# Seven half products in six pairs of chunks instead of three, and a new order, in an RWKV-6 mixer with an MLP

## The chip, the cores and the metric

The kernel runs on one core of a Trainium2 chip. The metric is the device time of one execution in microseconds (us). TensorE (PE) multiplies matrices, VectorE (DVE) and ScalarE (ACT) work on tiles and are the ones that read the accumulators (PSUM) that PE writes, GpSimd (POOL) works on tiles in SBUF, and SyncE (SP) issues the transfers (DMA). Each engine works through its own queue strictly in the order in which it was written; semaphores make it wait for others.

## The reference

```python
def _attn_ref(r, k, v, w, u):                 # [4, 8, 768, 48] each, u [8, 48]
    state = zeros(B, H, D, D)
    for t in range(S):
        cur = einsum('bhd,bhe->bhde', u * k[t], v[t])
        y[t] = einsum('bhd,bhde->bhe', r[t], state + cur)
        state = w[t][..., None] * state + einsum('bhd,bhe->bhde', k[t], v[t])
    return y
def _moe_ref(x, w_in, w_out):                 # x [3072, 384], w_in [384, 2048], w_out [2048, 384]
    h = x @ w_in
    g = np.maximum(0.01 * h, h)
    return g @ w_out
```

The y of the first part, its heads side by side, is the x of the second. Inputs and output are f32.

## The kernel before

**Chunks.** The 4 x 768 tokens are 24 chunks of 128, in an order in which consecutive chunks come from different batches, since the state passes from chunk to chunk of one batch. The first four chunks are done two at a time (`pair`, L537), the other twenty by `single` (L741). For one chunk of `single`: SP loads w, k, r and v (L755, 192 KB each) into one of ten buffers `in`; ACT takes the logarithm of w (L765); PE sums it along the tokens (L771, L774); DVE and ACT make from it the factors (L783, L792, L797, L801); DVE multiplies them with r and k (L459); the products are transposed, by PE with a copy out of PSUM (L470, L475, L477) or by a DMA transpose that SP issues (L818). PE then makes the scores (L912), DVE masks them (L842), PE multiplies them with v and adds the state's part (L878, L883). POOL makes the part of u (L489, L493, L501, with the sum L497 on DVE), casts v (L509) and scales the state (L829); DVE adds the part of u (L532), which gives y. y is transposed into xT by PE and a copy (L518, L523, L525) or by a DMA transpose that SP issues (L897).

**Blocks.** The MLP works on blocks of one or two chunks, listed in `blocks`. For a block, PE multiplies xT with w_in (the up-projection, L1074, 256 columns for a pair of chunks, 128 for a single one, six or twelve matmuls to a PSUM bank), and ACT makes g of it (L1089). Then g W_out follows in one of two forms:
- plain: per chunk 16 matmuls of 384 columns (L1104), a copy to `o` on DVE (L1115) or ACT (L1117), a store (L1121);
- seven products (`seven`, L963), for the last `SEVEN_LAST` blocks: g of a pair is cut into four quarters (two chunks, even and odd tiles of 128 features), w_out into four (even and odd tiles, left and right 192 columns). Four differences of quarters of w_out are made once on DVE (`mix`, L958). Per pair DVE makes four sums s1, s3, s2, s4 of quarters of g (L989), PE makes seven products of 8 matmuls with 192 columns (L1006) instead of eight, ACT or DVE takes three of them out of PSUM (L1020, L1022), and DVE adds five half rows into `o` (L1027: c11, f2, c21, c22, c12). The last pair makes its sums and its first products in two parts. The stores are issued at L1057.

**Order.** The kernel records about 1,100 steps, each with its engines, its estimated length and a rank, and a planner at build time (`Plan.order`) runs through them and writes the steps of each engine in the order that it finds. `RANK` adds a number to the rank of a step, and `FORCE` ties a step to one engine where several could do it. So both tables decide in what order the queues of all five engines stand, and which of DVE, ACT and POOL does a copy or a cast.

Of the kernel before, what the change touches and what calls it, by code (L numbers as in the profile page):

```python
# [23 lines left out]
class Plan:  # L24
# [138 lines left out]
RANK = {0: 15.37, 1: 14.4, 2: 3.33, 3: 23.03, 4: 38.76, 5: 12.01, 6: -26.8, 7: -21.87, 8: -21.96, 9: -19.05,  # L163
# [71 lines left out]
def kernel(  # L235
# [37 lines left out]
    SEVEN_LAST = 3  # L273
# [3 lines left out]
    blocks = [2, 1, 1, 1, 1, 2, 2, 2, 2, 2, 1, 1, 2, 2, 2]  # L277
# [903 lines left out]
```

## Time and profile before

| | |
|---|---|
| median of 3 runs | 181.93 us (181.49 to 182.0) |
| profiled execution | 181.35 us, span 179.6 us |
| busy: PE, DVE, ACT, POOL | 172.6, 132.2, 115.7, 104.0 us |
| granted TensorE clock | 1.00 |
| first up-projection, last matmul's group | starts at 19.78 us, 175.53 us |

The span goes from the first instruction to the last; the 1.75 us between it and the time of the execution lie around it. The profile gives, for each group of like instructions, its number, its busy time, the mean of one and the idle time of its engine before them. Matmuls overlap in the pipeline, so that the distance between starts says what one costs in a stream, not its mean.

### The profile page before, as it was taken

The numbers are of one execution on the slowest core, as the hardware profiler recorded it, in microseconds if no ns is written. First come the engines' busy times: TensorE is split into PE (matmuls) and PEld (weight loads), VectorE is DVE, ScalarE is ACT, GpSimd is POOL, SyncE is SP. The second block draws the span as 40 slices with busy tenths as digits, with TensorE's granted clock in tenths as the row PEclk, the third lists the DMA queues.
The fourth block names the chain that finished last, engine by engine and source line by source line (L and its number), as shares of the span: only waits on it lengthen the run. The fifth ranks groups of instructions, "written<-read, shape, count | busy, mean of one in ns | idle before, by whom it ended". The sixth has DMA issues, their size and how long they took to land.

```text
span 179.6 us, 5374 instructions
## 1 busy us (share of the span) xinstructions
PE 172.6 (96%) x2109; PEld 135.2 (75%) x2109; DVE 132.2 (74%) x265; ACT 115.7 (64%) x257; POOL 104.0 (58%) x138
## 2 busy tenths in 40 slices
PE   7998999999999999999999999999999999999991
PEld 2475878867878687787688777677778798899991
DVE  7589974189788898559687659499787599777472
ACT  2568968865957786895379775177675487735620
POOL 5989631675896486878468855414995459200000
PEclk9999999999999999999999999999999999999999
DMA  5999999999999989999899999999599996613004
GB/s 139 261 283 314 370 380 362 176 203 208 215 195 202 192 192 150 183 199 182 193 214 177 218 164 214 212 192 144 117 201 145 198 234 170 153 24 115 0 22 153
DMA packets 116715, 34.43 MB, mean 192 GB/s; under 512 B 109137, under 2 KB 115922, under 8 KB 116690
## 3 DMA queue, kind: packets, MB, share of 16 engines
q1 hardware_dynamic: 116688, 34.09, 90.8%
q8 instruction: 16, 0.26, 0.6%
q14 instruction: 9, 0.07, 0.1%
q10 hardware_dynamic: 2, 0.00, 0.0%
HBM read 25.17 MB, written 4.72 MB: 166 GB/s over the span
## 4 chain that ended last, share of the span: by engine, by line
PE 64%; DVE 8%; DMA 8%; ACT 6%; issue 5%; SPq 4%; POOL 3%; DVEq 0%; ACTq 0%; POOLq 0%
PE ps L1074 26%; PE ps L1104 17%; PE ps L1006 6%; DMA in<-in_w_dram 6%; SPq L755 3%; PE ps L1146 3%; PE ps L912 2%; DMA xT<-y 2%; DVE m L842 2%; POOL ru L489 1%; DVE o L1027 1%; ACT g L1089 1%; PE ps L883 1%; ACT rkT L477 1%; DVE m L690 1%
## 5 line engine op out<-in xcount | busy, mean ns | idle before, releaser
L1074 PE MATMUL ps<-xT,w_in_b 128*128 128x256 bf16 (+1 forms) x720 | 73.1, 251 | 0.4 <-ACT xT L525 0.2
L1089 ACT ACTIVATE g<-ps 128x512 bf16<-128x512 f32 x96 | 56.4, 595 | 20.6 <-PE ps L1074 15.3
L1074 PEld LDWEIGHTS <-w_in_b 128*128 128x128 bf16 x720 | 57.7, 98 | 9.3 <-issue 0.7
L1104 PE MATMUL ps<-w_out_b,g 128*128 128x384 bf16 x288 | 56.0, 326 | 0.1
L1104 PEld LDWEIGHTS <-g 128*128 128x128 bf16 x288 | 25.7, 97 | 12.4 <-ACT g L1089 0.2
L489 POOL TENSOR_TENSOR ru<-in,ub 128x384 f32<-128x384 f32 x24 | 24.5, 1027 | 10.9 <-DMA in<-in_k_dram 10.1
L459 DVE TENSOR_TENSOR rk<-in,ps 128x384 bf16<-128x384 f32 x46 | 24.3, 548 | 7.8 <-ACT ps L797 4.2
L842 DVE TENSOR_TENSOR m<-ps,maskb 128x512 bf16<-128x512 f32 x40 | 25.4, 683 | 6.1 <-PE ps L912 5.0
L493 POOL TENSOR_TENSOR ru<-ru,in 128x384 f32<-128x384 f32 x24 | 24.6, 1030 | 2.9 <-DMA in<-in_r_dram 2.2
L829 POOL TENSOR_TENSOR sb<-s,a 128x384 bf16<-128x384 f32 x18 | 15.7, 873 | 9.5 <-ACT a L792 9.4
L501 POOL TENSOR_TENSOR vs<-in,dg 128x384 f32<-128x384 f32 x20 | 16.6, 828 | 7.1 <-DVE dg L497 4.7
L509 POOL CAST vb<-in 128x384 bf16<-128x384 f32 x24 | 12.0, 503 | 11.3 <-DMA in<-in_v_dram 7.5
L783 DVE TENSOR_TENSOR ci<-ps,lw 128x384 f32<-128x384 f32 x20 | 11.1, 554 | 4.3 <-PE ps L771 1.9
L497 DVE TENSOR_REDUCE dg<-ru 128x8 f32<-128x384 f32 x24 | 12.9, 545 | 1.0 <-POOL ru L493 0.8
L765 ACT ACTIVATE lw<-in 128x384 bf16<-128x384 f32 x20 | 10.4, 520 | 3.6 <-DMA in<-in_w_dram 3.6
L797 ACT ACTIVATE ps<-ps 128x384 f32<-128x384 f32 x20 | 9.5, 475 | 4.2 <-DVE ci L783 3.8
L532 DVE TENSOR_TENSOR y<-ps,vs 128x384 bf16<-128x384 f32 x20 | 11.1, 553 | 1.5 <-PE ps L883 0.6
L867 DVE TENSOR_TENSOR s<-ps,sb 128x384 f32<-128x384 f32 x14 | 7.7, 552 | 4.0 <-PE ps L852 2.8
L801 ACT ACTIVATE ps<-ci 128x384 f32<-128x384 f32 x20 | 9.8, 488 | 0.6 <-DVE ci L783 0.6
L1146 PE MATMUL ps<-zeros 128*128 128x128 bf16 (+1 forms) x40 | 8.7, 339 | 1.3 <-DVE zeros L332 1.3
L525 ACT COPY xT<-ps 128x384 bf16<-128x384 bf16 x11 | 5.2, 481 | 6.8 <-PE ps L518 6.7
L792 ACT ACTIVATE a<-ps 64x4 f32<-64x4 f32 x36 | 6.0, 168 | 5.3 <-DVE ci L783 3.5
(105 smaller groups left out, 228.7 us busy)
## 6 DMA issues: line engine op xcount, KB each, us to landing
out_dram<-o SPq DMA_DIRECT2D x23, 192.0 KB, 3.2
in<-in_w_dram SPq DMA_DIRECT2D x20, 192.0 KB, 4.3
in<-in_k_dram SPq DMA_DIRECT2D x20, 192.0 KB, 4.2
in<-in_r_dram SPq DMA_DIRECT2D x20, 192.0 KB, 4.1
in<-in_v_dram SPq DMA_DIRECT2D x20, 192.0 KB, 4.3
in<-in_moe_w_out_dram SPq DMA_DIRECT2D x4, 768.0 KB, 12.3
in<-in_moe_w_in_dram SPq DMA_DIRECT2D x4, 384.0 KB, 7.0
in<-in_moe_w_in_dram SPq DMA_DIRECT2D x2, 768.0 KB, 9.8
```

The lines of the kernel that those rows point to most:

```text
L459: (nc.gpsimd if e == "POOL" else nc.vector).tensor_tensor(out=o, in0=x, in1=i, op=ALU.mult)
L489: lambda e: nc.gpsimd.tensor_tensor(out=ru.t[:], in0=kv(), in1=ubv, op=ALU.mult),
L493: lambda e: nc.gpsimd.tensor_tensor(out=ru.t[:], in0=ru.t[:], in1=rv(), op=ALU.mult),
L497: lambda e: nc.vector.tensor_reduce(out=dg.t[:], in_=ru.t[:], axis=AX.X, op=ALU.add),
L501: lambda e: nc.gpsimd.tensor_tensor(out=vs.t[:], in0=vv(), in1=dg.t[:].unsqueeze(2).to_broadcast([128, H, D]), op=ALU.mult),
L509: {"POOL": 0.56}, lambda e: nc.gpsimd.tensor_copy(out=vb.t[:], in_=vv()),
L829: lambda e: nc.gpsimd.tensor_tensor(out=sb.t[:].rearrange("p g a d -> p (g a) d"), in0=s_in.t[:].rearrange("p g a d -> p (g a) d"), in1=a_ ...
L842: lambda e, par=par: nc.vector.tensor_tensor(out=m.t[:, par, :, :], in0=sc[par].t[:].rearrange("p (g t) -> p g t", g=NP), in1=maskb[:].uns ...
L1074: nc.tensor.matmul(hp.t[:, a * N : (a + 1) * N], lhsT=w_in_b[:, t, (j + a) * 128 : (j + a + 1) * 128], rhs=xT[:, t, c0 : c0 + N], start=(a ...
L1089: lambda e, hp=hp, g=g, j=j, J=J, N=N: nc.scalar.activation(out=g.t[:, j : j + J, 0:N], in_=hp.t[:, 0 : J * N].rearrange("p (a n) -> p a n ...
L1104: nc.tensor.matmul(op.t[:, 0:DM], lhsT=g.t[:, j, off : off + 128], rhs=w_out_b[:, j, :], start=(j == 0), stop=(j == NJ - 1))
L1146: nc.tensor.matmul(warm.t[:, 0:n], lhsT=zeros[:, 0:128], rhs=zeros[:, 0:n], start=True, stop=True, skip_group_check=True)
```

## The change

Two numbers change in the kernel's body: the last six blocks, not the last three, use the seven products, and the two single blocks of chunks 16 and 17 become one pair, so that the six last blocks are pairs.

```diff
-    SEVEN_LAST = 3
+    SEVEN_LAST = 6
...
-    blocks = [2, 1, 1, 1, 1, 2, 2, 2, 2, 2, 1, 1, 2, 2, 2]
+    blocks = [2, 1, 1, 1, 1, 2, 2, 2, 2, 2, 2, 2, 2, 2]
```

The tables of the order are replaced as a whole, `RANK` with a number for nearly every step instead of for about half of them (the numbers of the steps of the MLP shift with the blocks):

```diff
-RANK = {0: 15.37, 1: 14.4, 2: 3.33, 3: 23.03, 4: 38.76, 5: 12.01, 6: -26.8, 7: -21.87, 8: -21.96, 9: -19.05,
...
+RANK = {0: -94.4, 1: -32.42, 2: -177.44, 3: -177.74, 4: 23.17, 5: -227.73, 6: -32.49, 7: -32.59, 8: -32.69, 9:
...
-FORCE = {23: "DVE", 26: "DVE", 29: "ACT", 30: "DVE", 46: "ACT", 58: "ACT", 61: "ACT", 79: "ACT", 85: "DVE",
...
+FORCE = {5: "ACT", 29: "DVE", 30: "DVE", 32: "DVE", 46: "ACT", 59: "ACT", 61: "DVE", 79: "ACT", 82: "ACT", 85:
...
```

What the two programs issue, where it differs:

| | before | after |
|---|---|---|
| L1006, 192 columns (PE) | 168 | 336 |
| L1104, 384 columns (PE) | 288 | 192 |
| L1074, 256 and 128 columns (PE) | 432 and 288 | 480 and 192 |
| L989, sums of g (DVE) | 16 | 28 |
| L1027, half sums (DVE) | 15 | 30 |
| L1115 on DVE, L1117 on ACT | 7, 11 | 2, 10 |
| L1020 on DVE, L1022 on ACT | 2, 7 | 1, 17 |
| L475 on DVE, L477 on ACT | 9, 13 | 11, 11 |

The lines of the changed kernel stand 78 further down (L1074 is L1152 there); the text goes by those of the kernel before. The pairs that use the seven products are chunks 18/19, 20/21 and 22/23 before, and all from 12/13 to 22/23 after.

More of the change, by code (lines that the diff above doesn't have):

```diff
@@ L162 @@
 TY = (0.95, 24, 0.7, -0.6)
-RANK = {0: 15.37, 1: 14.4, 2: 3.33, 3: 23.03, 4: 38.76, 5: 12.01, 6: -26.8, 7: -21.87, 8: -21.96, 9: -19.05,
[63 rows of a table removed]
-FORCE = {23: "DVE", 26: "DVE", 29: "ACT", 30: "DVE", 46: "ACT", 58: "ACT", 61: "ACT", 79: "ACT", 85: "DVE",
-    112: "DVE", 114: "ACT", 117: "DVE", 119: "ACT", 121: "ACT", 123: "DVE", 125: "POOL", 127: "ACT", 128:
-    "POOL", 134: "POOL", 137: "DVE", 139: "POOL", 142: "ACT", 143: "POOL", 492: "DVE", 500: "ACT", 604: "DVE",
-    612: "ACT", 904: "DVE", 910: "DVE", 932: "ACT", 952: "ACT", 966: "ACT", 1002: "ACT", 1030: "ACT", 1075:
-    "ACT", 1080: "ACT"}
+RANK = {0: -94.4, 1: -32.42, 2: -177.44, 3: -177.74, 4: 23.17, 5: -227.73, 6: -32.49, 7: -32.59, 8: -32.69, 9:
[138 rows of a table added]
+FORCE = {5: "ACT", 29: "DVE", 30: "DVE", 32: "DVE", 46: "ACT", 59: "ACT", 61: "DVE", 79: "ACT", 82: "ACT", 85:
+    "DVE", 86: "DVE", 112: "DVE", 114: "ACT", 115: "ACT", 117: "DVE", 127: "POOL", 128: "ACT", 130: "DVE",
+    131: "POOL", 134: "POOL", 140: "DVE", 142: "ACT", 159: "DVE", 168: "ACT", 172: "ACT", 186: "DVE", 188:
+    "ACT", 197: "ACT", 201: "DVE", 237: "DVE", 239: "DVE", 253: "ACT", 261: "DVE", 277: "ACT", 308: "DVE",
+    340: "ACT", 342: "ACT", 435: "DVE", 443: "DVE", 492: "ACT", 604: "ACT", 612: "ACT", 736: "ACT", 742:
+    "ACT", 756: "DVE", 784: "ACT", 798: "ACT", 826: "ACT", 876: "ACT", 910: "ACT", 913: "ACT", 946: "ACT",
+    949: "ACT", 982: "ACT", 985: "ACT", 990: "ACT", 1018: "ACT", 1021: "ACT", 1026: "ACT", 1054: "DVE", 1062:
+    "ACT", 1096: "ACT", 1099: "ACT", 1104: "ACT"}
 @with_exitstack
```

201 rows, old and new, of the table RANK are left out of this document.

## The prediction

> **What bounds the kernel now.** I read the page first, then the busy time of the engines by stage, then the groups of instructions by shape, and last the order of time on single engines. The page:
>
> ```profile
> PE 172.6 (96%) x2109; PEld 135.2 (75%) x2109; DVE 132.2 (74%) x265; ACT 115.7 (64%) x257; POOL 104.0 (58%) x138
> ...
> PE   7998999999999999999999999999999999999991
> ...
> PEclk9999999999999999999999999999999999999999
> ...
> PE 64%; DVE 8%; DMA 8%; ACT 6%; issue 5%; SPq 4%; POOL 3%; DVEq 0%; ACTq 0%; POOLq 0%
> ```
>
> TensorE (PE) is busy in every slice from the first to the last but one, at the full clock, and most of the chain that ended last is PE. A busy PE need not be a PE at its pace, so I ask next how often it stood idle, and what the other engines do in the same stages:
>
> ```profile
> 80.00:100.00 20.00, 19.88 (x240) 15.52 (x238) 15.88 (x32) 13.31 (x32) 13.62 (x18) 1.00 0.98 192
> 100.00:120.00 20.00, 20.00 (x211) 14.70 (x210) 14.00 (x26) 10.75 (x26) 10.11 (x13) 1.00 1.09 196
> 120.00:140.00 20.00, 19.92 (x260) 15.67 (x259) 16.60 (x30) 13.41 (x34) 14.24 (x16) 1.00 0.98 158
> 140.00:160.00 20.00, 19.91 (x249) 16.64 (x245) 15.77 (x28) 12.94 (x29) 9.26 (x12) 1.00 0.75 161
> ...
> L1104 PE MATMUL ps<-w_out_b,g 128*128 128x384 bf16 x288 | 56.0, 326 | 0.1
> L1074 PE MATMUL ps<-xT,w_in_b 128*128 128x256 bf16 x432 | 54.1, 272 | 0.4 <-ACT xT L525 0.2
> ```
>
> The columns after the length of a stretch are PE, weight loads, VectorE (DVE), ScalarE (ACT) and GpSimd (POOL). PE is full; VectorE is next with 46.4 of the 60 us from 100 to 160, 77%. The two big groups of matmuls waited 0.5 us in all. So from the first product with w_in (19.8 us) on, the end is set by the sum of PE's work, as long as the others keep ahead of it.
>
> **The change part by part.** *PE's work.* The mean of a matmul in a group is its way through the pipeline; what it costs in a full stream is the distance from one start to the next:
>
> ```profile
> 117.67 0.62 PE L912 MATMUL ps<-rkT 48*128 48x128 bf16 x16
> 118.22 1.48 PE L1074 MATMUL ps<-xT,w_in_b 128*128 128x256 bf16 x12
> ...
> 124.09 0.33 PE L878 MATMUL ps<-sb,rkT 128*128 128x96 bf16 x4
> 124.27 0.36 PE L883 MATMUL ps<-vb,m 128*128 128x48 bf16 x8
> 124.47 0.32 PE L771 MATMUL ps<-lw,trev 128*128 128x384 bf16 x1
> ...
> 124.73 3.41 PE L1104 MATMUL ps<-w_out_b,g 128*128 128x384 bf16 x20
> 127.98 0.83 PE L1074 MATMUL ps<-xT,w_in_b 128*128 128x128 bf16 x12
> 128.65 0.33 PE L852 MATMUL ps<-vb,rk 128*128 128x96 bf16 x4
> 128.82 0.83 PE L1074 MATMUL ps<-xT,w_in_b 128*128 128x128 bf16 x12
> ...
> 160.54 0.82 PE L1006 MATMUL ps<-in,in 128*128 128x192 bf16 x8
> 161.20 0.82 PE L1006 MATMUL ps<-in,g 128*128 128x192 bf16 x8
> ...
> 163.18 3.44 PE L1074 MATMUL ps<-xT,w_in_b 128*128 128x256 bf16 x30
> 166.46 0.82 PE L1006 MATMUL ps<-in,g 128*128 128x192 bf16 x8
> ```
>
> A 384-column product of the old kind (L1104) costs (127.98 − 124.73)/20 = 0.1625 us, a 192-column product of the seven (L1006) 0.66/8 = 0.0825, an up-projection of 256 columns 3.28/30 = 0.1093 and of 128 columns 0.67/12 = 0.0558. Three more pairs of chunks go from the plain form to the seven products: 3 × 32 = 96 of L1104 go (−15.60 us), 3 × 56 = 168 of L1006 come (+13.86). Chunks 16 and 17, single blocks before, become one: 96 narrow up-projections go (−5.36), 48 wide ones come (+5.25). Together −1.85 us of 160, and PE has nothing to hide it behind. This is the firm term.
>
> The Trainium skill (TensorE: Matmul & The Clock Gate, Back-to-back issue gap) speaks against it: in a stream in which each matmul has its weight load, it gives about 81 ns a matmul at 128 columns and 131 at 512. An estimate on the straight line between them is 89 ns for 192, 114 for 384, 98 for 256, so the edit would add 168 × 89 − 96 × 114 − 96 × 81 + 48 × 98 = +0.9 us instead. The trace does not agree: 55.8 ns at 128 columns and 82.5 at 192.
>
> *VectorE's work.* Per pair of chunks the seven products add four sums over g (L989, 128x1024) and five sums of halves into o (L1027); copies of o (L1115) go. In the changed order VectorE has 12 more sums, 15 more L1027 and 5 fewer L1115; the four differences of w_out (L958) come earlier, among chunks 10 to 13. What they cost beside each other:
>
> ```profile
> 143.05 2.48 DVE L842 TENSOR_TENSOR m<-ps,maskb 128x512 bf16<-128x512 f32 x4 [1.50 <-PE ps L912]
> 145.55 0.56 DVE L532 TENSOR_TENSOR y<-ps,vs 128x384 bf16<-128x384 f32 x1
> 146.02 0.55 DVE L783 TENSOR_TENSOR ci<-ps,lw 128x384 f32<-128x384 f32 x1
> 146.49 0.54 DVE L497 TENSOR_REDUCE dg<-ru 128x8 f32<-128x384 f32 x1
> ...
> 151.51 1.35 DVE L989 TENSOR_TENSOR g<-g 128x1024 bf16<-128x1024 bf16 x1
> ...
> 162.13 0.69 DVE L989 TENSOR_TENSOR g<-g 128x1024 bf16<-128x1024 bf16 x1
> 162.74 0.61 DVE L1027 TENSOR_TENSOR o<-ps,o 128x192 f32<-128x192 f32 x2
> 163.27 0.68 DVE L989 TENSOR_TENSOR in<-in,g 128x1024 bf16<-128x1024 bf16 x1
> ...
> 151.48 0.83 POOL L829 TENSOR_TENSOR sb<-s,a 128x384 bf16<-128x384 f32 x1
> ```
>
> A 384-column step costs 0.47 us (145.55 to 146.02 to 146.49), a mask 0.62, here 0.6, a half sum 0.27, here 0.28. The same sum took 0.69 us alone and 1.35 when it started beside GpSimd's L829; I price it at 0.84, nearer to the lone rows, and keep 0.6 and 1.35 as ends.
>
> I then count the queue of VectorE from y of chunk 13 to the last y (chunks 22 and 23), and PE's from the first up-projection of chunks 12/13 to that of 22/23. Before: 91 instructions, by these prices 48 us, beside 64 us of PE: 75%. After: 108 (20 masks, 54 steps of 384, 16 sums, 16 half sums, two copies into xT), 56 us. PE there has 40 groups of six wide up-projections (26.2), 32 sets of eight L1006 (21.1), 28 L1104 (4.6) and 10.7 us of small work, 62.5: VectorE is at 90%. The tightest place is behind the seven products of chunks 12/13. Their last half sum waits for PE's last product, and behind it in VectorE's queue stand 25 instructions up to y of chunk 18: 13 steps (6.1 us), 4 masks (2.4), 4 half sums (1.1), 4 sums (3.4), 13.0 us. In the same time PE goes through 9 up-projection groups (5.9), nine sets of eight L1006 (5.9) and small work of chunks 18 to 21 (L912 0.55, L878 with L883 0.38, twice L771 and what follows it 0.26, L852 0.17: 1.6), 13.4 us, and then needs that y to transpose it. Slack of 0.4 us, less the handovers, is nothing: PE waits if any of it slips. Upper end: the five sums up to y of chunk 19, all at 1.35, are 2.5 us. Lower end: −0.3, since the wide groups waited only 0.5 in the whole run. I take **+0.8 us**, a third of the upper end, for this and the like places before chunks 20/21 and 22/23; they do not add up, for a PE that waits lets VectorE gain on it.
>
> *The start.* PE's first up-projection waits for xT of both first chunks, which ACT makes last:
>
> ```profile
> 16.26 0.83 ACT L415 CAST w_in_b<-in 128x768 bf16<-128x768 f32 x1
> ...
> 17.84 0.50 ACT L734 CAST y<-ps 128x384 bf16<-128x384 f32 x1
> ...
> 18.86 0.87 ACT L525 COPY xT<-ps 128x384 bf16<-128x384 bf16 x2
> ...
> 19.78 1.47 PE L1074 MATMUL ps<-xT,w_in_b 128*128 128x256 bf16 x12
> ```
>
> After, ACT copies both y (L734) before its casts of w_in, and VectorE makes one of the two xT. That takes the cast of 0.83 and half of 0.87 out of the chain, 1.2 us at most; late is then VectorE, which does five products, a reduction and two transposed copies behind its masks before its xT, and the casts of w_in that now follow. I take **−0.5**, ends −1.0 and 0. Between 24 and 100 us PE's work is the same; loads and transposes stand in another order in SP's queue. I put nothing there, since PE waited for none of it in the row of L1074.
>
> *The end.* The last sum of halves, then a store:
>
> ```profile
> 176.39 0.36 DVE L1027 TENSOR_TENSOR o<-ps,o 128x192 f32<-128x192 f32 x1 [0.65 <-PE ps L1006]
> ...
> out_dram<-o SPq DMA_DIRECT2D x5, 192.0 KB, 1.9
> out_dram<-o SPq DMA_DIRECT2D x2, 96.0 KB, 1.6
> ```
>
> Before, the last store is a half (96 KB); after, c21 comes last and its store is whole: **+0.3 us**. PE's work behind the last up-projection stays at 6.6 us.
>
> *Sum*, on the profiled execution (181.35 us, span 179.6): 181.35 − 1.85 − 0.5 + 0.8 + 0.3 = 180.1. That execution lies 0.58 under the median of the three runs (181.93), so the time to expect of a median is **180.7 us**.
>
> **Rivals.** *VectorE becomes the bound* (slower). Place: chunks 14 to 23. For it: 90% of PE's time by rather kind prices, with each half sum waiting for a product in the middle of the same queue, and GpSimd busy for 47.2 of 80 us in the four stages above. Against: the stretch decides only from 62.5 us on, so 6.5 us of slip must come together. Price: 16 sums at 1.35 instead of 0.84 are 8.2 us, to 64.3; 2 us of waits for products and ACT make 66.3, so 3.8 us of PE standing: 180.7 − 0.8 + 3.8 = 183.7. The Trainium skill (GPSIMD Engine Reference, 1. Specifications) says that GpSimd shares its SBUF interfaces with VectorE when an instruction of the latter has two inputs there; the 1.35 beside 0.69 agrees.
>
> *The new order gives the gain back* (no change). A transpose issued by SP waits for its y or rk, and what stands behind it in that queue, loads and other transposes, waits along. One such wait of the 0.7 us by which a lone sum and one beside GpSimd differ would already outlast the slack; with nothing gained at the start, 180.7 + 0.5 + 0.7 = 181.9.
>
> *Start and middle both turn out well*: −1.0 at the start, −0.3 instead of 0.8 in the middle: 180.7 − 0.5 − 1.1 = 179.1.
>
> *The weight loads set the pace* of the seven products, so that the change saves nothing on PE. Their record is longer than the distance of the matmuls:
>
> ```profile
> L1006 PEld LDWEIGHTS <-g 128*128 128x128 bf16 x96 | 8.0, 98 | 0.5 <-ACT g L1089 0.4
> ```
>
> 168 × 0.098 = 16.5 for 15.6 is +0.9 where the sum has 13.86 − 15.60 = −1.7, so 180.7 + 2.6 = 183.3. Against it stand the 0.66 us of eight, loads included. The rule of the page on TensorE above is this rival.
>
> **How the numbers follow.** Forecast 0.58, both well 0.06, order gives it back 0.12, VectorE the bound 0.22, weight loads 0.02. A measurement of this kernel tells about 0.3% from no change, 181.4 to 182.5. So faster 0.64, same 0.12, slower 0.24. The forecast's own ends (−1.0 − 0.3 at one side, 0 and +2.5 at the other) are 179.1 and 182.9. The range for 8 in 10 goes from 178.9, under the good case, to 183.8, just over the price of the VectorE case, whose dearer half it leaves out.
>
> **What would show it.** 336 of L1006 at 0.66 us for eight, 192 of L1104: the firm term. The first up-projection before 19.5 us: the start. In the stages from 100 to 160 VectorE above 17 of 20 us, PE still above 19.7: the forecast; PE at 19 with idle put down to y or xT: the VectorE rival. L989 with a mean over 1.1 us would confirm its price. Idle on PE put down to rkT or xT by DMA would be the order's. The forecast is wrong if PE loses over 1.5 us between 100 and 165, or if the up-projections wait for weights before 36 us.

## The result and the profile after

The changed kernel takes 182.81 us (median of 20 runs, 181.37 to 185.3) beside 181.56 for the kernel before in the same measurement (20 runs, 180.32 to 183.06): a ratio of 1.007 with a 95% interval of 1.0041 to 1.0098. It is slower by 0.7%, some 1.25 us. The forecast was 180.7 us and faster. The profiled execution of the changed kernel took 182.09 us, its span 180.4. The quoted lines of the changed kernel stand 78 lower than before: L1152 is the up-projection (before L1074), L1182 the plain product (L1104), L1084 the seven products (L1006), L1067 the sums of g (L989), L1105 the half sums (L1027), L1100 the takes (L1022), L1167 the activation into g (L1089), L861 ci, L870, L875 and L879 ScalarE's exponentials, L833 the loads, L537 the products into rk, L990 the scores.

The page of the changed kernel: busy time, the row of forty slices of the DMA engines, the transfer queue, and the chain that ended last.

```profile
PE 169.2 (94%) x2126; PEld 137.8 (76%) x2126; DVE 143.3 (79%) x286; ACT 116.9 (65%) x266; POOL 106.4 (59%) x138
...
DMA  5999999998999999799998999998979978522031
...
q1 hardware_dynamic: 116688, 34.09, 91.0%
...
PE 63%; DVE 14%; DMA 7%; issue 4%; ACT 3%; POOL 3%; SPq 3%; DVEq 0%; ACTq 0%; POOLq 0%
```

PE has less work (busy 169.2 for 172.6) and the end is no earlier. VectorE's part of the chain went from 8% to 14%. The row to read twice is DMA: with few exceptions the 16 engines are at least nine tenths busy from the second slice to past 140 us, and the times of the one queue's packets add up to 91% of the 16 engines' span. It was 90.8% before, on the page that the prediction read; the prediction passes over it.

The stages from 100 us on (PE, weight loads, VectorE, ScalarE, GpSimd, clock, DMA share):

```profile
100.00:120.00 20.00, 19.72 (x252) 16.30 (x251) 17.55 (x32) 13.42 (x33) 13.02 (x16) 1.00 1.09 211
120.00:140.00 20.00, 19.21 (x247) 17.08 (x246) 18.26 (x37) 13.37 (x35) 10.33 (x13) 1.00 0.92 170
140.00:160.00 20.00, 20.00 (x249) 18.04 (x250) 17.87 (x35) 13.21 (x30) 12.72 (x14) 1.00 0.74 163
```

VectorE is at 53.7 of 60 us where it had 46.4. Of these stages PE stands idle most in the one from 120 to 140. What it waited for, in the whole run:

```profile
PE ps L548 <- DVE rk L537: 1.6, 2, 0.8
...
PE ps L930 <- POOL vb L587: 1.0, 2, 0.8
...
PE ps L1084 <- DVE o L1105: 0.7, 1, 0.7
PE ps L1084 <- ACT o L1100: 0.7, 1, 0.7
```

These are some of many small waits in different places, none of these over 0.8 us. Two can be followed by eye. In order of time, on PE and on GpSimd, with the start of the run's up-projections:

```profile
19.59 1.49 PE L1152 MATMUL ps<-xT,w_in_b 128*128 128x256 bf16 x12
...
62.69 0.33 PE L930 MATMUL ps<-vb,rk 128*128 128x96 bf16 x4 [0.77 <-POOL vb L587]
...
129.22 0.82 PE L1084 MATMUL ps<-in,in 128*128 128x192 bf16 x8 [0.66 <-ACT o L1100]
...
62.13 0.50 POOL L587 CAST vb<-in 128x384 bf16<-128x384 f32 x1 [1.99 <-DMA in<-in_v_dram]
```

At 62.69 PE waits 0.77 us for GpSimd's cast of v, which itself waits for a load. At 129.22 it waits 0.66 us for ScalarE to empty a bank of products, and that copy stands in ScalarE's queue behind work that waits for VectorE, as the experiments show. The sums themselves did not grow dear (groups of VectorE by shape):

```profile
L1067 DVE TENSOR_TENSOR in<-g,in 128x1024 bf16<-128x1024 bf16 x5 | 5.3, 1051 | 0.0
L1067 DVE TENSOR_TENSOR in<-in,g 128x1024 bf16<-128x1024 bf16 x5 | 4.1, 817 | 0.0
L1067 DVE TENSOR_TENSOR in<-g 128x1024 bf16<-128x1024 bf16 x5 | 3.8, 752 | 0.0
L1067 DVE TENSOR_TENSOR g<-g 128x1024 bf16<-128x1024 bf16 x5 | 3.4, 680 | 0.0
```

16.6 us for 20 sums are 0.83 us each; 0.84 was the price taken. So the sizes on VectorE were right and the time still went.

### The profile page after: what moved, and what is told of

Same layout as the page of the kernel before. It is cut to its first block, busy times and chain, and to the rows that moved or that the text cites. A ratio compares the mean times of both kernels' runs of the same rounds, so it can differ in the third digit from the quotient of the medians.

```text
span 180.4 us, 5448 instructions
## 1 busy us (share of the span) xinstructions
PE 169.2 (94%) x2126; PEld 137.8 (76%) x2126; DVE 143.3 (79%) x286; ACT 116.9 (65%) x266; POOL 106.4 (59%) x138
## 2 busy tenths in 40 slices
DMA packets 116716, 34.43 MB, mean 191 GB/s; under 512 B 109137, under 2 KB 115922, under 8 KB 116690
## 4 chain that ended last, share of the span: by engine, by line
PE 63%; DVE 14%; DMA 7%; issue 4%; ACT 3%; POOL 3%; SPq 3%; DVEq 0%; ACTq 0%; POOLq 0%
PE ps L1152 26%; PE ps L1084 12%; PE ps L1182 11%; DMA in<-in_v_dram 5%; DVE rk L537 3%; SPq L833 3%; PE ps L1224 2%; DMA out_dram<-o 2%; PE ps L990 2%; DVE m L920 2%; POOL vb L587 2%; PE ps L961 2%; DVE in L1067 2%; DVE o L1105 2%; DVE rkT L553 1%
## 5 line engine op out<-in xcount | busy, mean ns | idle before, releaser
L1152 PE MATMUL ps<-xT,w_in_b 128*128 128x256 bf16 (+1 forms) x672 | 72.5, 257 | 0.3 <-ACT g L1167 0.3
L1167 ACT ACTIVATE g<-ps 128x512 bf16<-128x512 f32 x96 | 55.8, 596 | 17.2 <-PE ps L1152 13.4
L1152 PEld LDWEIGHTS <-w_in_b 128*128 128x128 bf16 x672 | 56.1, 98 | 7.7 <-issue 0.8
L1182 PE MATMUL ps<-w_out_b,g 128*128 128x384 bf16 x192 | 36.8, 326 | 0.0
L537 DVE TENSOR_TENSOR rk<-in,ps 128x384 bf16<-128x384 f32 x46 | 24.0, 549 | 7.6 <-ACT ps L675 2.5
L571 POOL TENSOR_TENSOR ru<-ru,in 128x384 f32<-128x384 f32 x24 | 25.7, 1079 | 4.4 <-DMA in<-in_r_dram 4.3
L1182 PEld LDWEIGHTS <-g 128*128 128x128 bf16 x192 | 17.3, 98 | 8.7
L587 POOL CAST vb<-in 128x384 bf16<-128x384 f32 x24 | 14.4, 602 | 9.0 <-DMA in<-in_v_dram 9.0
L1084 PEld LDWEIGHTS <-g 128*128 128x128 bf16 x192 | 15.8, 98 | 0.2
L861 DVE TENSOR_TENSOR ci<-ps,lw 128x384 f32<-128x384 f32 x20 | 11.0, 552 | 3.6 <-PE ps L849 2.3
L1084 PEld LDWEIGHTS <-in 128*128 128x128 bf16 x144 | 12.1, 98 | 1.8 <-issue 1.7
L1105 DVE TENSOR_TENSOR o<-ps,o 128x192 f32<-128x192 f32 x30 | 10.1, 350 | 4.1 <-PE ps L1084 3.5
L1100 ACT COPY o<-ps 128x192 f32<-128x192 f32 x17 | 5.4, 318 | 11.7 <-PE ps L1084 7.6
L870 ACT ACTIVATE a<-ps 64x4 f32<-64x4 f32 x36 | 6.1, 168 | 8.0 <-DVE ci L861 6.4
L1084 PE MATMUL ps<-in,in 128*128 128x192 bf16 x96 | 9.9, 246 | 1.4 <-DVE o L1105 0.7
L879 ACT ACTIVATE ps<-ci 128x384 f32<-128x384 f32 x20 | 9.7, 487 | 2.2 <-DVE ci L861 2.2
```

Source lines behind the costliest of these rows:

```text
L537: (nc.gpsimd if e == "POOL" else nc.vector).tensor_tensor(out=o, in0=x, in1=i, op=ALU.mult)
L571: lambda e: nc.gpsimd.tensor_tensor(out=ru.t[:], in0=ru.t[:], in1=rv(), op=ALU.mult),
L587: {"POOL": 0.56}, lambda e: nc.gpsimd.tensor_copy(out=vb.t[:], in_=vv()),
L1084: nc.tensor.matmul(o(), lhsT=x()[:, i, :], rhs=y()[:, i, :], start=fresh, stop=(stop and i == ii[-1]), skip_group_check=True)
L1105: nc.vector.tensor_tensor(out=o(), in0=y(), in1=x(), op=ALU.add)
L1152: nc.tensor.matmul(hp.t[:, a * N : (a + 1) * N], lhsT=w_in_b[:, t, (j + a) * 128 : (j + a + 1) * 128], rhs=xT[:, t, c0 : c0 + N], start=(a ...
```

## The experiments

Two theories stood at first. **V**: VectorE's longer queue makes other engines, and through them PE, wait. **O**: the newly searched order and its stores cost the time. The first runs called for a third, **D**: the transfer queue is a second bound, so that time taken out of PE's work is waited back for loads. All ratios are to the kernel before, measured on the same chip in the same measurement, with 95% intervals; 0.001 is 0.18 us. The difference of two ratios is good to 0.5 to 0.7 us. The changed kernel itself was measured only once, in the first row; a_tail and a_mend, which differ little from it, came out close to it on two other chips.

| kernel | ratio | interval |
|---|---|---|
| changed kernel | 1.0070 | 1.0041–1.0098 |
| b_pe12: before, 12 products fewer | 0.9994 | 0.9971–1.0018 |
| a_pe24: changed, 24 half-width products fewer | 0.9991 | 0.9967–1.0014 |
| a_light: changed, sums on one tile | 1.0001 | 0.9973–1.0030 |
| a_tail: changed, last output stored in halves | 1.0087 | 1.0059–1.0115 |
| b_nor: before, no loads of r | 0.9987 | 0.9970–1.0003 |
| b_nor_pe12: before, without both | 0.9894 | 0.9871–0.9917 |
| b_tinyr_pe12: 12 fewer, tiny loads of r | 0.9871 | 0.9857–0.9885 |
| a_nor: changed, no loads of r | 0.9980 | 0.9964–0.9996 |
| a_nor_light: a_nor, sums on one tile | 0.9887 | 0.9864–0.9910 |
| a_nor_pad: a_nor_light, the rest of each sum behind it | 1.0055 | 1.0033–1.0077 |
| a_nor_take: a_nor, one copy moved | 0.9962 | 0.9947–0.9977 |
| a_mend: changed, a copy and a load moved | 1.0054 | 1.0029–1.0079 |
| b_nor_dve: b_nor, more VectorE work | 1.0275 | 1.0247–1.0304 |
| b_norank: before, order not searched | 1.0207 | 1.0180–1.0235 |
| a_norank: changed, order not searched | 1.0865 | 1.0829–1.0901 |
| a_pool: a_mend, a sum on GpSimd | 1.0106 | 1.0069–1.0143 |

### Is a microsecond of PE's work worth a microsecond?

```
-                        for j in range(q * NJ // 4, (q + 1) * NJ // 4):
+                        for j in [j for j in range(q * NJ // 4, (q + 1) * NJ // 4) if j != 5 or not 4 <= ch < 16]:
```

> The kernel before, with one of the 16 matmuls of L1104 left out in each of chunks 4 to 15 (their product with w_out lacks one 128-row term): 12 x 0.1625 = 1.95 us less work on PE, no other instruction changed on any engine. Theory W (PE's work sets the end of the kernel before, as the prediction said): -1.95 us, 0.989 of the time before. Theory S (PE's queue stands so often for work of other engines that less work on PE turns into waits): -0.5 us or less, 0.997 or more.

The kernel before without 1.95 us of PE's work: 0.9994. The work is gone and the time is not: theory W falls for this stretch, the plain products of chunks 4 to 15. The profiled execution shows places where the time can go. It took 181.78 us, the longest of twelve with a median of 180.40, so its waits are examples and not the mean. In order of time on PE, and one row of SP's queue:

```profile
53.30 0.33 PE L852 MATMUL ps<-vb,rk 128*128 128x96 bf16 x4 [0.86 <-POOL vb L509]
...
88.46 0.62 PE L912 MATMUL ps<-rkT 48*128 48x128 bf16 x16
90.61 1.47 PE L1074 MATMUL ps<-xT,w_in_b 128*128 128x256 bf16 x12 [1.53 <-DMA xT<-y]
...
81.13 3.20 SPq L818 DMA_TRANSPOSE rkT<-rk  x1
```

At 53.30 PE waits for GpSimd's cast of v, which had waited 0.96 us for v's load. In the kernel before, the same up-projection started at 89.53, without a wait:

```profile
88.80 0.62 PE L912 MATMUL ps<-rkT 48*128 48x128 bf16 x16
89.53 1.47 PE L1074 MATMUL ps<-xT,w_in_b 128*128 128x256 bf16 x12
...
81.95 1.34 SPq L818 DMA_TRANSPOSE rkT<-rk  x1
```

PE reaches the place 0.34 us earlier and leaves it 1.1 us later, because a transposed y has not landed: the transpose ahead of it held SP's queue for 3.20 us, for 1.34 before. Whether the transfers as such are what takes the time back is tested below. The queue's share on the page does not tell: it is 96.9% here, and goes from 87.0% to 96.9% over the profiled executions with the same bytes, and does not follow their times.

```
-                        for i in ii:
+                        for i in [i for i in ii if at != 8.5 or i % 2 == 0]:
```

> The changed kernel, with four of the eight matmuls of the product of s2 left out in each of the six seven-product blocks (half of that product's terms are missing): 24 x 0.0825 = 1.98 us less on PE from about 100 us on, nothing else changed. Theory V (VectorE's longer queue sets the pace of the changed kernel from 100 us on): the matmuls left out are replaced by waits, 0 to -0.6 us against the changed kernel, 1.004 to 1.007 of the time before. Theory O (VectorE has room; the searched order and the stores cost the time): PE's work is worth its length, -2 us against the changed kernel, 0.996 of the time before.

0.9991, 1.4 us under the changed kernel: between the two numbers expected. PE's work from 100 us on is worth most of its length, with all the loads in the kernel, and this is the stretch where the change takes work off PE: its first product of the seven starts at 110.46 us. So b_pe12 says nothing against the firm term in its own place. Three of the six shortened products start behind 144 us, where the loads run out (DMA share 0.74 from 140 to 160 in the changed kernel).

### Is the transfer queue the second bound?

```
-                    nc.sync.dma_start(out=part(i)(), in_=src[b, :, t0 : t0 + L, :].rearrange("h p d -> p h d"))
+                    i != 2 and nc.sync.dma_start(out=part(i)(), in_=src[b, :, t0 : t0 + L, :].rearrange("h p d -> p h d"))
...
-            wv, kv, rv, vv = (part(i) for i in range(4))
+            wv, kv, rv, vv = (part(i) for i in (0, 1, 0, 3))
```

> The kernel before without the 20 loads of r for chunks 4 to 23 (192 KB each, 3.9 of 34 MB moved); w stands in for r in the three operations that read it, so their values differ and nothing else does. Theory D (the one DMA queue, with its 16 engines full from 20 to 150 us, is a second bound beside PE: a us taken from PE's work there is waited back for transfers): faster by what PE waits for in that stretch, -1 to -3 us, 0.983 to 0.995 of the time before. Theory S (waits come from the order alone, each engine standing behind another): 0 to -0.5 us.

> The kernel before without the loads of r and without the 12 matmuls of L1104 as well. Theory D: with the queue no longer full, PE's work has its whole worth again: 1.4 to 1.95 us under the kernel that only lacks the loads. Theory S: within 0.5 us of it, as it was with all the loads.

Without the loads alone: 0.9987, hardly a change, under the −1 us that theory D put at the least. Without the 12 products alone: 0.9994. Without both: 0.9894, which is 1.9 us, and 1.7 us under the kernel without the loads. So neither is *the* bound. Each covers for the other, as D says in its core; that PE waited much for transfers in the kernel before, as D's first number had it, is wrong. The page of b_nor shows what room the queue got, and the chain:

```profile
q1 hardware_dynamic: 95888, 30.16, 78.6%
...
PE 76%; DVE 7%; ACT 5%; DMA 5%; issue 2%; POOL 2%; SPq 1%; DVEq 0%; ACTq 0%
```

PE's part of the chain is 76% for 64% in the kernel before. By itself that says little: a_mend below has 80% with all the loads, and b_tinyr_pe12, the fastest of all, 67%.

Against b_nor_pe12:

```
-                    i != 2 and nc.sync.dma_start(out=part(i)(), in_=src[b, :, t0 : t0 + L, :].rearrange("h p d -> p h d"))
+                    p = 1 if i == 2 else L
+                    nc.sync.dma_start(out=part(i)()[0:p], in_=src[b, :, t0 : t0 + p, :].rearrange("h p d -> p h d"))
```

> The kernel before without the 12 matmuls of L1104 and with w in place of r, as before, but with the 20 loads of r still issued by SP, each of one token (1.5 KB) instead of 128 (192 KB). Theory D by data (the 16 engines are full of the loads' packets): as without the loads, 0.989 of the time before. Theory D by issue (SP's queue, each transfer's place and turn in it): as with all loads, 0.997 to 1.000.

0.9871: with the 20 transfers still issued, but small, the time is that of the kernel without them. What fills up is the engines with the loads' data, not SP's turn to issue. The edit takes away the waits for r itself as well, and no run tells these apart from the rest of the queue; the waits seen on PE above are for v and for a transposed y. The loads are made of pieces of 48 floats. The page of the changed kernel has the speed in 40 slices and the sizes:

```profile
GB/s 144 261 273 328 369 380 360 179 197 178 195 155 192 186 200 170 152 198 220 194 182 165 227 174 243 181 207 175 210 146 156 233 178 179 139 46 88 0 109 67
DMA packets 116716, 34.43 MB, mean 191 GB/s; under 512 B 109137, under 2 KB 115922, under 8 KB 116690
```

109137 of 116716 packets are under 512 B. The Trainium skill (DMA: Bandwidth & Descriptors, Specifications) gives 512 B as the least size for full rate. The trace agrees: from 20 to 30 us, where the weights are loaded, 79 of 2447 packets are under 512 B and the queue moves 375 GB/s; from 50 to 60 us 8790 of 8791 are, and it moves 174. The slices from 32 to 140 us have 146 to 243 GB/s, with the engines busy in nearly all of them.

### What VectorE's queue costs

```
-                            out=o()[:, i0:i1], in0=in0()[:, i0:i1], in1=in1()[:, i0:i1], op=op)
+                            out=o()[:, i0:i0 + 1], in0=in0()[:, i0:i0 + 1], in1=in1()[:, i0:i0 + 1], op=op)
...
-                                o(), lhsT=x()[:, i, :], rhs=y()[:, i, :], start=fresh, stop=(stop and i == ii[-1]),
+                                o(), lhsT=x()[:, 0 if at in (8.5, 12.5, 14.5) else i, :], rhs=y()[:, i, :], start=fresh, stop=(stop and i == ii[-1]),
```

> The changed kernel with each of the sums of g (L1067) on the first of its eight (or four) tiles alone, and the products that take them reading that tile eight times (these three products of each block are not those of the reference): VectorE's 28 sums, 4 of them of halves in two, go from about 0.83 us to about 0.2 us each, some 15 us less on VectorE from 100 us on, and the number of instructions on every engine and their order stay. Theory V: PE's waits from 100 to 170 us go, -1.5 to -2.5 us against the changed kernel, 0.993 to 0.998 of the time before. Theory O: 0 to -0.5 us, 1.004 to 1.007.

1.0001, 1.25 us under the changed kernel: V has a part, and not all.

> The changed kernel without the loads of r, w in their place. Theory D: the queue held back the seven products' saving of 1.85 us, so without its load the changed kernel stands 1 to 2 us under the kernel before without the same loads. Theory V (VectorE's longer queue): it stays about 1.2 us above it. Between the two if both hold.

> The changed kernel without the loads of r and with the sums of g on one of their eight tiles (three products of each of the six blocks read that tile eight times). Theory D alone: within 0.5 us of the changed kernel without the loads. Theory V: 1 to 2 us under it.

The changed kernel without the loads of r is at 0.9980, level with the kernel before without them (0.9987): these loads cost the changed kernel 1.4 us more than the kernel before. With the sums lightened too it is at 0.9887, 1.8 us under the kernel before without the loads, close to the firm term of the prediction, 1.85. VectorE's load is then about that of the kernel before: busy 130.5 us, where a_nor has 141.6 and b_nor 131.5. Both theories are needed: about 1.4 us for D and 1.7 us for V.

Where D's part falls can be read from the traces of the changed kernel and of a_nor, which have the same order. Two rows of the changed kernel, on PE:

```profile
89.69 0.33 PE L930 MATMUL ps<-vb,rk 128*128 128x96 bf16 x4 [0.19 <-POOL vb L587]
...
110.46 1.48 PE L1084 MATMUL ps<-w_out_b,g 128*128 128x192 bf16 x16
```

In a_nor the products of 62.69 and 89.69 start at 61.68 and 88.34, without a wait: the changed kernel is 1.01 us behind at the first and 1.35 at the second, of which 0.16 stood before 60 us, and 1.30 at the last product. So all of it is lost by 90 us, before the first product of the seven at 110.46. It is not time saved on PE that is waited back, but a loss where PE has the same work as before, in a new order of the loads. These are single executions, of 182.09 and 180.19 us, but the wait is not: the one for vb at 62 us is in the profiled executions of all four kernels with all loads in this order (0.77 to 1.09 us: the changed kernel, a_light, a_tail, a_pe24), in none without the loads of r, and in neither of the two with that load of v moved forward (a_mend, a_pool).

Without the loads the place of V can be seen. The changed kernel without the loads (a_nor), VectorE, then ScalarE, then PE, in order of time:

```profile
123.57 1.04 DVE L1067 TENSOR_TENSOR in<-g 128x1024 bf16<-128x1024 bf16 x1
...
124.99 0.68 DVE L1067 TENSOR_TENSOR g<-g 128x1024 bf16<-128x1024 bf16 x1
125.59 0.54 DVE L861 TENSOR_TENSOR ci<-ps,lw 128x384 f32<-128x384 f32 x1
...
127.59 1.40 DVE L1067 TENSOR_TENSOR in<-g,in 128x1024 bf16<-128x1024 bf16 x1
...
126.23 0.35 ACT L870 ACTIVATE a<-ps 64x4 f32<-64x4 f32 x2 [1.10 <-DVE ci L861]
...
127.51 0.32 ACT L1100 COPY o<-ps 128x192 f32<-128x192 f32 x1
...
127.88 0.82 PE L1084 MATMUL ps<-in,in 128*128 128x192 bf16 x8 [0.67 <-ACT o L1100]
...
132.18 0.78 PE L990 MATMUL ps<-rkT 48*128 48x128 bf16 x16
```

Read it backwards. PE waits 0.67 us for ScalarE's copy; the copy stands behind three exponentials; these wait 1.10 us for ci; ci stands on VectorE behind two sums. PE's product with the second of them starts at 125.74, that with the first only at 130.77. With the sums lightened (a_nor_light) ci and the same rows of PE are:

```profile
124.66 0.56 DVE L861 TENSOR_TENSOR ci<-ps,lw 128x384 f32<-128x384 f32 x1
...
127.05 0.82 PE L1084 MATMUL ps<-in,in 128*128 128x192 bf16 x8
...
131.35 0.62 PE L990 MATMUL ps<-rkT 48*128 48x128 bf16 x16
...
171.84 0.82 PE L1084 MATMUL ps<-w_out_b,in 128*128 128x192 bf16 x8
172.50 0.82 PE L1084 MATMUL ps<-in,g 128*128 128x192 bf16 x8
```

ci is 0.93 us earlier, PE 0.83 us at both places. The last product of a_nor starts at 174.20, 1.70 later than here; up to 124.4 the two run alike. Of the 1.70 us, 1.38 are there by 136.3 us, and the kernel before (b_nor) has its first sum at 148.3; so at most 0.3 us can come from sums that it has too. The kernel before with its own sums lightened was not run.

```
...
+                        rest = sv({"s1": 0, "s3": 1, "s2": 1, "s4": 2}[name])[:, i0 + 1:i1]
+                        nc.vector.tensor_tensor(
+                            out=rest, in0=a(0, 0)[:, i0 + 1:i1], in1=a(0, 1)[:, i0 + 1:i1], op=ALU.add)
```

> The changed kernel without the loads of r, with each sum of g done on its first tile alone, as in the lightened kernel, and right behind it on VectorE an addition of the other seven (or three) tiles whose result no instruction reads. VectorE has its full work again, but no product waits for the long part. Theory Q (what is queued behind the sums on VectorE comes late): back to the changed kernel without the loads of r, 0.996 to 0.999 of the time before. Theory P (the products wait for their sums): as fast as the lightened one, 0.988 to 0.990.

1.0055. The products no longer wait for the long part of the sums, and the price is back, and 1.4 us more, since 28 instructions were added and a full-width sum in two parts takes longer than in one:

```profile
L1070 DVE TENSOR_TENSOR in<-g 128x896 bf16<-128x896 bf16 x20 | 15.7, 784 | 0.0
...
L1067 DVE TENSOR_TENSOR in<-g 128x128 bf16<-128x128 bf16 x7 | 1.9, 269 | 1.7 <-ACT g L1170 1.7
```

That is 0.784 + 0.269 us against 0.83 (the lines behind L1067 stand 3 further down in this kernel). It is the queue (theory Q), not the products' wait for their operands.

```
-        order = plan.order(pools)
+        order = moved(plan.order(pools))
...
+def moved(order):
+    for i, j in ((946, 621),):
+        order.remove(i)
+        order.insert(order.index(j), i)
+    return order
```

> The changed kernel without the loads of r, and with one ScalarE copy moved: the take of the first product of chunks 16/17 (L1100) stands ahead of chunk 19's L870, L875 and L879 instead of behind them, which wait for VectorE's ci. Theory Q places 0.66 us of PE's idle time at 129 us there (PE's next product needs the bank that this copy empties): -0.6 to -0.8 us against the changed kernel without the loads, 0.994. If the wait only moves to the next operation, 0 and 0.998.

0.9962: 0.3 us less, half of what was expected, and within the error. The rows say why (a_nor_take, the same engines):

```profile
127.57 1.40 DVE L1067 TENSOR_TENSOR in<-g,in 128x1024 bf16<-128x1024 bf16 x1
...
127.03 0.82 PE L1084 MATMUL ps<-in,in 128*128 128x192 bf16 x8
128.06 0.32 PE L849 MATMUL ps<-lw,trev 128*128 128x384 bf16 x1 [0.21 <-ACT lw L843]
...
132.25 0.68 PE L990 MATMUL ps<-rkT 48*128 48x128 bf16 x8 [0.15 <-DVE rk L537]
```

PE's product starts 0.85 us earlier, at 127.03, and by the scores (L990) nothing is left of it: 132.25, for which PE waits on rk. VectorE's rows are where they were, to 0.02 us. Here the wait that VectorE's queue ended came back at the next thing that this queue delivered.

```
-                lambda e: nc.vector.tensor_tensor(out=y.t[:], in0=heads(yp.t), in1=vs.t[:], op=ALU.add),
+                lambda e: [nc.vector.tensor_tensor(out=y.t[:], in0=heads(yp.t), in1=vs.t[:], op=ALU.add)] + [nc.vector.tensor_tensor(out=zeros[:], in0=w_in_b[:, 0, x : x + 512], in1=w_in_b[:, 1, x : x + 512], op=ALU.add) for x in (0, 512) if 90 <= P0 < 210],
```

> The kernel before without the loads of r (w in their place) and with two additions of 128x512 bf16 on VectorE behind the sum of y of each of chunks 9 to 20, 24 in all of about 0.42 us (10 us, from some 75 to 155 us), whose results no instruction reads. The change adds 11 us to VectorE. Theory Q: VectorE's time there has a price without anything else of the change, 1 to 2 us over the kernel without the loads: 1.005 to 1.010 of the time before. If the price lies in the seven products' own order or banks: 0 to 0.4 us, 0.999 to 1.001.

1.0275, 5.2 us over b_nor, far more than the 1 to 2 expected. The 24 additions took 14.0 us instead of 10 (group of VectorE):

```profile
L532 DVE TENSOR_TENSOR zeros<-w_in_b 128x512 bf16<-128x512 bf16 x24 | 14.0, 582 | 0.4
```

So VectorE's time has a price in the kernel before too, 0.37 us a us at this place, on the way from y to xT and on an order that was not made for it. The change's 11 us cost 1.7, 0.15 a us, in an order that was. This shows that there is a price, not that the two prices have one cause.

### Is it the new order?

```
-            done = [(ob, chs[1], 0, DM, [s_c21, s_c22])]
+            if nb == len(blocks) - 1:
+                done = [(ob, chs[1], HN, DM, [s_c22]), (oa, chs[0], 0, HN, [s_c11]), (oa, chs[0], HN, DM, [s_c12]),
+                        (ob, chs[1], 0, HN, [s_c21])]
```

> The changed kernel with chunk 23's output stored in two halves, each as soon as its half is summed, instead of one whole store after the last sum. Nothing else changes. Both theories: the last store moves 96 KB instead of 192 KB; -0.3 us (the prediction's price of that store) to -0.8 us (what the span of the changed kernel has after its last sum over that of the kernel before): 1.003 to 1.005 of the time before. If the end of the span hangs on the queue's own latency, 0.

1.0087: no gain. In the profiled execution the last sum ends at 178.08 and the span 3.3 us later, instead of 3.7. The smaller store's 0.4 us is less than the runs of this kernel differ among each other (181.52 to 183.12), and a_mend, with the whole store, has 3.3 us there too.

```
+    for i, j in ((946, 621), (265, 293)):
```

> The changed kernel, all loads in it, with two moves: the same ScalarE copy, and the load of chunk 8's v on SP ahead of chunk 9's w instead of behind that and two loads of r. The two waits in its profile are 0.66 us (at 129 us) and 0.77 us (at 62.7 us). If each is worth its length: -1.4 us, 0.999 of the time before. Theory D says that the load's wait moves to a later transfer, since the queue stays full: -0.7 us, 1.003.

1.0054: −0.3 us where two waits of 1.4 us were taken out of the rows (PE's list of waits has neither L587's cast nor L1100 any more). The copy's gain is lost again by 134 us in the trace, as above. The load's is not: in the profiled execution PE is 1.0 us ahead of the changed kernel from 90 us on, and 1.1 at the end. That execution took 180.68 us, the shortest of twelve with a median of 181.36; where the others lose it is not known.

```
-        for i, x in RANK.items():
+        for i, x in {}.items():
...
-        for i, e in FORCE.items():
+        for i, e in {}.items():
```

> The kernel before without the searched ranks and engine choices: the planner's own priorities alone order the work. Slower by an amount that no theory gives; it is the base for the next.

> The changed kernel without the searched ranks and engine choices. If the change as such costs time (VectorE's queue and the full transfer queue, theories Q and D), it stands within 1 us of, or above, the kernel before in the same state. If the new searched order is what costs (theory O), the seven products show their 1.85 us here: 1.5 to 2 us under it.

1.0207 and 1.0865: without the search the changed kernel stands 12 us over the kernel before, also unsearched. Theory O falls as it was put: the seven products show no gain when the searched orders are gone, and the search takes 14 us off the changed kernel and 4 off the kernel before. That does not clear every part of the new order; its loads before 90 us cost time, as shown above. Unsearched, PE waits more, for the sums themselves too (a_norank, waits of PE):

```profile
PE ps L1152 <- DMA xT<-y: 3.2, 2, 2.0
PE ps L596 <- DVE y L610: 2.8, 2, 1.5
PE ps L1084 <- DVE in L1067: 2.1, 4, 1.0
```

Two planner orders are only two samples, and the granted clock of a_norank is 0.983, so the 12 us is no clean price of the change.

```
-                        nc.vector.tensor_tensor(
+                        eng.tensor_tensor(
```

(eng is nc.gpsimd for the fourth sum of the five full blocks, nc.vector otherwise.)

> The changed kernel with the two moves (the ScalarE copy, chunk 8's load of v) and with the fourth sum of five of the six blocks done by GpSimd at the same place of the order. VectorE loses 5 sums of about 1.05 us, GpSimd gets 5 that its 1.0 us for 384 floats puts at 1 to 2.7 us each. Theory Q: a third of VectorE's price comes back, -0.5 us against the kernel with the two moves, 1.002 of the time before. Against it: GpSimd's own queue stands longer before casts of v and sb, and slows VectorE's sums beside it: 1.006 or more.

1.0106, 0.9 us over a_mend. VectorE is down to 137.0 us busy, but GpSimd's sum takes 2.12 us:

```profile
L1067 POOL TENSOR_TENSOR in<-g,in 128x1024 bf16<-128x1024 bf16 x5 | 10.6, 2124 | 6.2 <-DVE in L1067 6.2
```

GpSimd stands 6.2 us before these five for VectorE's third sum, with casts of v and products for vs behind it, and its part of the chain is 17%, for 0% in a_mend. No version here beats the kernel before with the reference's whole work in it.

## Why the prediction was wrong, step by step

- *"The end is set by the sum of PE's work, as long as the others keep ahead of it."* The condition failed. It was read from PE's busy 96%, from the full clock and from 0.5 us of waits in the two big groups. A row without waits says that nothing is late now; it does not say by how much. 1.95 us less work for chunks 4 to 15 in the kernel before brought 0.1 us, and 1.7 without the loads of r: the loads were as close behind as PE. In the sum this failed at two terms, the stretch from 24 to 100 us, put at nothing, and VectorE's.
- *The firm term, −1.85.* Its size is right: L1084 goes at 0.66 us for eight (171.84 to 172.50 in the lightened kernel's rows), −1.8 us comes out when the loads of r and most of the sums' load are both gone, and with all loads 1.4 of 1.98 us taken off PE in the same stretch came through (a_pe24). It is there in the changed kernel, under two losses that together are larger.
- *VectorE, +0.8.* The mechanism named is the one that happened: sums ahead of other steps in VectorE's queue, with PE at the end of a chain through ScalarE. Its size was 1.25 (a_light) to 1.7 (a_nor_light), inside the ends of −0.3 to +2.5. The choice of a third of the upper end rested on "a PE that waits lets VectorE gain on it"; the moved copy shows the other side, that a gain of PE is lost to VectorE again. Nor was it at y of chunk 18 as counted, but at ci of chunk 19, since the count took the queue's length and not which step in it was wanted first.
- *The VectorE rival, 183.7.* The side was right, and as a change it was the nearest: +1.8 us over the 181.93 it was counted from, for +1.25 measured. That is in part luck, for its price came from sums at 1.35 us and had nothing for the loads. The sums took 0.83; the sign asked of it, a mean over 1.1, did not show.
- *"Between 24 and 100 us … I put nothing there."* This step failed most: about 1.4 us by the ratios, and 1.35 in the traces by 90 us, 0.85 of it at the late load of 62.7 us. The prediction names that loads and transposes stand in another order and puts nothing there, since PE had waited for none of it in one row before; that was taken for slack.
- *The start, −0.5.* The first up-projection came at 19.59 instead of 19.78, and not before 19.5. It moves from execution to execution, 18.98 to 19.84 us in those with the order of before and 18.56 to 19.59 in those with the new one, so one pair of profiles cannot show this term; no gain of 0.5 us is seen.
- *The end, +0.3.* In the profiled executions the span runs 3.7 us past the last sum for 2.9 before, 0.8 more; but with the same whole store it is 3.1 us in a_nor, and halving that store brought nothing measurable.
- *Rival "the new order gives the gain back".* It forecast no change, 1.25 us from the result, and its price was for one wait behind a transpose. Its mechanism, transfers in a new order of SP's queue that hold up what stands behind them, is near to what the traces show before 90 us. That loss needs both: without the loads of r the same order does not have it, and with them the order of before loses only 0.2 us to them.
- *The signs.* VectorE was above 17 of 20 us in all three stages, as forecast. PE idled 1.1 us between 100 and 165, under the 1.5 named as the sign of a wrong forecast: that sign left out the stretch before 100 us, where the loads' part was lost.
- *Rival "weight loads".* PE's distances are as priced; it is out.

Sum with what the runs showed: −1.8 (PE), +1.4 (loads), +1.7 (VectorE) are +1.3, beside 1.25 measured. That the sum closes is no proof: the three terms are differences along one chain of the same ratios, and add up to the result by their making. What they show is their sizes. What stays open is how the loads' 1.4 splits over its places in other executions than the two compared, and whether another searched order would avoid it.

## What to carry to other kernels

Before you count a saving on the busiest engine, count the second and third resource over the whole run, the transfer queue among them, and over the stretches where the work stays the same but its order changes. A busy share or a chain of one execution does not show how close they are: PE was 96% busy, and its part of the chain went from 44% to 88% over these kernels without following their times. To test it, take work off one resource, then off the other, then off both. Then compare two traces of the same order instruction by instruction, which shows where the time is lost and whether the saved work stands there at all. A wait that is removed by moving one instruction only counts if the queue that ended it is not the one that ends the next.

## What the runs showed of the hardware

- With nearly all packets under 512 B the 16 engines moved 146 to 243 GB/s in the slices from 32 to 140 us of the changed kernel, with hardly any of them 375 GB/s (20 to 30 us). SP issued 20 more tiny transfers at no cost that shows (0.9871 with, 0.9894 without).
- A sum of 128x1024 took longer where GpSimd worked beside it, and GpSimd too. In a_nor the sum at 127.59, quoted above, took 1.40 us; the sum of the same size at 124.99, with GpSimd waiting, took 0.68. GpSimd's rows there:

```profile
126.66 0.83 POOL L907 TENSOR_TENSOR sb<-s,a 128x384 bf16<-128x384 f32 x1 [2.60 <-ACT a L870]
127.44 1.00 POOL L567 TENSOR_TENSOR ru<-in,ub 128x384 f32<-128x384 f32 x1
128.40 2.41 POOL L571 TENSOR_TENSOR ru<-ru,in 128x384 f32<-128x384 f32 x2
```

  Its last two took 2.41 us together, and 1.96 at the same place with the sums lightened.
- The same addition of 1024 bf16 takes 0.68 us on VectorE and 2.12 on GpSimd.
